# Attention and feed-forward in one kernel: casts, a shift of V and two V products placed at other half-steps

## The chip, the cores and the metric

The kernel runs on one core of a Trainium2 chip. The metric is the device time of the whole program in microseconds (us). A core has five engines that run side by side, each working off its own queue strictly in order: TensorE (PE, matmuls), VectorE (DVE), ScalarE (ACT), GpSimd (POOL, which also issues DMAs) and SyncE (SP, which only issues DMAs). They wait for one another through semaphores.

## What is computed

Sliding-window causal attention over 8 batches, 8 heads, 576 positions and head size 64, and behind it a feed-forward layer without residual:

```python
scores = scale * np.matmul(q, k.transpose(0, 1, 3, 2))
mask = (rel >= 0) & (rel < window)          # rel = query - key position, window = 64
attn = softmax(np.where(mask, scores, -1e9))
x = np.matmul(attn, v)                      # as 4608 tokens x 512
h = x @ w_in                                # 512 -> 2048
out = (h - np.tanh(h)) @ w_out              # 2048 -> 512
```

## The kernel before

**Attention.** Heads are worked on in pairs: pair g is pair g mod 4 of batch g // 4, so there are 32 of them, 4 to a batch. A window of 64 queries needs 128 keys, and a batch has 9 windows. Loads by POOL's DMA queue turn float32 into bf16 on their way (`kall`, `qall`, `vall`). For a pair, `cast` (L111) reorders k and q into `kb` and `qb`; PE transposes them (`tr_rows`, L264) and an engine copies the result out to `kt` and `qs`. `tile_scores` (L279) makes the scores in two groups of windows (5 and 4), ACT takes the exponential (`pt`), and, with "mask", DVE multiplies by the mask (L295). `tile_pv` (L297) multiplies by V, and DVE divides by the row sums (reciprocal L308, product L310, into `xs`). For later pairs `scores`, `masking`, `pv` (L328) and `norm` (L335) do the same with other tiles. `x_tr` turns `xs` into the token-last form `xT`. V takes its own road: `cast_v` (L159) into `vb`, nine DMAs `keys_v` (L163) from `vb` into the upper 64 partitions of the window tile `vw`, half of them issued by SP and half by POOL, and then a shift of the upper into the lower partitions, one window on (`shift_v`, L168; by DVE in two copies of 64x2080 elements, L171).

**Feed-forward.** Tokens go in 9 chunks of 512. For a chunk, 16 h products (`hp_mm`, L377, four matmuls 128x512 each) fill a PSUM bank each, ACT takes the tanh (L388), and `g_sub` (L391) subtracts on DVE into `gT` (L395), which frees the bank. In chunk 1 three banks serve in turn (`hp_bank`, L374), and the tanh output has three buffers: the fourth h product waits for the first one's subtraction. Four y products to a token tile (`yp_mm`, L407) and `y_out` finish the chunk.

**The order.** It is written out by hand on a time scale of half-steps h. The dictionary `OPS` gives each half-step at most one h or y product: chunk 0 has h product m at half-step 2m, chunk 1 at 32 + 2m, chunk 0's y parts are at 64 to 79. `at(h, fn, ...)` hangs attention work on a half-step. The loop at the end emits, for each h: the h or y product (PE and tanh), then the hung items in the order in which `at` named them, then the subtraction. Below, "gT m" is the subtraction of h product m of its chunk. The order of the calls is the order on every engine's queue; nothing is rescheduled.

The lines that matter here: `cast_v` of batch 1 (L524), the casts of pairs 4 to 11 (L527 to L562), `shift_dve` of batch 2 (L563), the row of pair 8 in the table of L536 to L541 (its four numbers are the half-steps of the k transpose, the q transpose and the two groups of scores), `tile_pv` of pairs 8 and 9 (L564, L565), and `pv` and `norm` of the loop over later pairs (L597, L599; for pair 10, a = 49).

Of the kernel before, what the change touches and what calls it, by code (L numbers as in the profile page):

```python
# [15 lines left out]
def kernel(  # L16
# [142 lines left out]
    def cast_v(b, pr, eng=nc.gpsimd):  # L159
        move(eng, vb[:, :, 2 * pr:2 * pr + 2, 0:D].rearrange("p e h d -> p h e d"),  # L160
             stage.pop((b, pr, "v")).rearrange("p h (e d) -> p h e d", d=D))

    def keys_v(b, j, eng=nc.sync):  # L163

        eng.dma_start(out=vw[b % 2][64:128, j].rearrange("p h c -> p (h c)"),  # L165
                      in_=vb[8 * j:8 * j + 8].rearrange("p e h c -> p e (h c)"))
# [274 lines left out]
    def at(h, fn, *args):  # L441
        items.setdefault(h, []).append((fn, args))
# [10 lines left out]
    V, A, G, Y = nc.vector, nc.scalar, nc.gpsimd, nc.sync  # L453
# [67 lines left out]

    at(0, lambda: nc.vector.memset(vw[1][0:64, 0], 0.0))
    at(0, lambda: nc.vector.memset(qT[1], 0.0))
    for pr, h in enumerate((1, 3, 5, 9)):  # L524
        at(h, cast_v, 1, pr, V)
    at(9, lambda: [keys_v(1, j, (G, Y)[j % 2]) for j in range(NJ)])
    at(8, cast_pair, 4, V)  # L527
    at(11, cast_pair, 5, V)
    at(9, load_v_all, 2)
    for g in 8, 9, 10, 11:  # L530
# [5 lines left out]
    for g, t, ka, qa, a, b, eng in ((4, (10, 11, 13, 14), 6, 7, (4, 5), (6, 7), V),  # L536
                                    (5, (13, 14, 16, 17), 2, 3, (4, 5), (6, 7), V),
                                    (6, (17, 18, 20, 22), 2, 3, (4, 5), (4, 5), A),
                                    (7, (20, 22, 24, 26), 3, 3, (4, 5), (4, 5), A),
                                    (8, (31, 32, 34, 36), 3, 5, (4, 5), (4, 5), A),  # L540
                                    (9, (37, 38, 42, 44), 3, 6, (4, 5), (4, 5), A)):  # L541
        at(t[0], tr_rows, g, "k", ka, eng)
        at(t[1], tr_rows, g, "q", qa, A)
        at(t[2], tile_scores, g, 0, a, "hide" if g < 8 else "mask")
        at(t[3], tile_scores, g, 1, b, "hide" if g < 8 else "mask")
# [4 lines left out]
    at(30, x_tr, 1, 1, 0, 4, 7, V)  # L550
    at(30, x_tr, 1, 1, 4, 9, 4, A)
    at(21, lambda: [cast_v(2, pr) for pr in range(NP)])
    at(21, cast_pair, 8, G)
    at(23, lambda: [keys_v(2, j, (G, Y)[j % 2]) for j in range(NJ)])
    at(33, cast_pair, 9, V)
    at(23, load_w_out, 0)
    at(23, load_w_out, 1)
    at(23, load_all, 3, "q")
# [1 line left out]
    at(23, load_v_all, 3)  # L560
    at(44, cast_pair, 10, G)
    at(50, cast_pair, 11, G)  # L562
    at(39, shift_dve, 2, 0, 4)  # L563
    at(44, tile_pv, 8, (6, 7))  # L564
    at(48, tile_pv, 9, (6, 7))  # L565
    at(53, x_tr, 2, 0, 0, 4, 6, V)
    at(55, x_tr, 2, 0, 4, 9, 7, A)
# [7 lines left out]
    for g in range(2 * NP + 2, B * NP):  # L575
        b, pr = divmod(g, NP)
        a = STEPS[b][pr] if b in STEPS else 8 * g - 36
        if b == B - 1:
            at(a - 28, pace, a - 28)
            at(a - 28, load, g, "q", G)  # L580
            at(a - 28, load, g, "k", G)
            at(a - 17, cast, g, "q")
            at(a - 16, cast, g, "k")
            at(a - 14, bounce, g, "q")
            at(a - 13, bounce, g, "k")
            at(a - 8, tr_dma, g, "q")
            at(a - 7, tr_dma, g, "k")
            at(a, spread, g)
        elif b > 2:
            at(a - 7, cast, g, "q")  # L590
            at(a - 5, cast, g, "k")
        if b < B - 1:
            at(a, tr, g, "q", 5 if g < 12 else 2 if g < 13 else 3, A, V)
            at(a + 2, tr, g, "k", 3, A)
        for i in range(3):
            at(a + 5 + 2 * i, scores, g, i, 4)
            at(a + 13 + i, pv, g, i)  # L597
        at(a + 11, masking, g)
        at(a + 15, norm, g)  # L599
        if g in TURNS:  # L600
            h0, b0, h1, b1 = TURNS[g]
            at(h0, x_tr, b, pr // 2, 0, 4, b0, V)
            at(h1, x_tr, b, pr // 2, 4, 9, b1, A)
        elif b > 3 and pr == NP - 1:
            at(a + 16, x_dma, b)
        if b > 2:
            cv, cs, ky = VALUES[b]
            at(cv + cs * pr, cast_v, b, pr)
        if pr == 0 and b > 2:
            for j in range(NJ):  # L610
                if b == 3:
                    at(ky, windows_v, b, j, (G, Y)[j % 2])
                else:
                    at(ky + j // 2 if b < 7 else ky + j, windows_v if b < 5 else keys_v, b, j, Y)
            if b > 4:
                at(ky + 7 if b < 7 else ky + 11, shift_v, b, 0, NJ - 1)
            if b == 3:
                continue
            hk, hq, hv = LOADS[b]
            for h, f in sorted(((hq, (load_all, b, "q")), (hk, (load_all, b, "k")), (hv, (load_v_all, b))),  # L620
                               key=lambda x: x[0])[2 if b == B - 1 else 0:]:
                at(h, pace, h)
                at(h, *f)
# [49 lines left out]
```

## Time and profile before

| what | value |
|---|---|
| median of five runs | 335.81 us (334.38 to 336.46) |
| the profiled execution's own time | 334.5 us |
| its span on the core | 332.8 us |
| PE busy | 315.4 us, 95% of the span |
| DVE busy | 198.7 us, 60% |
| ACT busy | 184.0 us, 55% |
| POOL busy | 114.8 us, 34% |
| 50 to 57 us: PE, DVE, ACT, POOL busy | 6.83, 5.06, 6.63, 7.00 of 7.00 us |
| 57 to 61 us: the same | 3.04, 3.94, 3.11, 4.00 of 4.00 us |
| 61 to 65 us: the same | 3.30, 3.97, 1.44, 1.53 of 4.00 us |

The profile is of one execution. Times in it count from the start of the span. A line of its timeline has the start, the duration, the engine, the source line and operation, the output and inputs, and in brackets how long the engine was idle before and who ended the wait.

### The profile page before, as it was taken

What the parts mean: (1) busy time and instruction counts of PE and PEld (TensorE: products, weight loads), DVE (VectorE), ACT (ScalarE), POOL (GpSimd) and SP (SyncE); (2) the same over time, 40 slices, a digit from 0 to 9 for tenths busy, and PEclk for the clock granted to TensorE, in tenths of its full rate; (3) what the DMA queues carried; (4) which work ended last, traced back from release to release, by engine and by line L of the source; (5) the groups of instructions that cost most, each with busy time, mean ns of one, the idle gap of its engine ahead of it and who ended that gap; (6) DMA issues with size and microseconds to landing.
All of it is one profiled execution on the core that took longest, in us unless ns stands there. A gap on an engine that the chain in (4) does not pass through costs nothing.

```text
span 332.8 us, 6238 instructions
## 1 busy us (share of the span) xinstructions
PE 315.4 (95%) x2408; PEld 176.5 (53%) x2439; DVE 198.7 (60%) x335; ACT 184.0 (55%) x337; POOL 114.8 (34%) x167
## 2 busy tenths in 40 slices
PE   6788999899999999999999999999999999999996
PEld 2564565465555655555555555555554444444444
DVE  4588597983257675767676666776666433344400
ACT  3545879583565666766556666555553444434411
POOL 8853589505920843532723493400000000000000
PEclk9569999999999999999999999999999999999999
DMA  8999996994797289475976968967104001100022
GB/s 159 166 194 207 165 187 104 200 194 97 123 194 143 44 153 224 90 113 130 166 134 115 156 146 162 199 145 166 63 32 102 34 32 42 53 33 32 32 84 77
DMA packets 47222, 40.68 MB, mean 122 GB/s; under 512 B 18632, under 2 KB 40584, under 8 KB 47000
## 3 DMA queue, kind: packets, MB, share of 16 engines
q0 software_dynamic: 21440, 19.73, 39.1%
q1 hardware_dynamic: 25544, 20.25, 24.1%
q8 instruction: 19, 0.31, 0.4%
q10 hardware_dynamic: 208, 0.29, 0.3%
q14 instruction: 11, 0.09, 0.1%
HBM read 36.70 MB, written 10.62 MB: 142 GB/s over the span
## 4 chain that ended last, share of the span: by engine, by line
PE 71%; DMA 10%; DVE 9%; POOL 3%; ACT 3%; issue 2%; POOLq 0%; DVEq 0%
PE ps L407 32%; PE ps L383 28%; DMA vall<-in_v_dram 4%; DMA vw<-vb 3%; DMA qall<-in_q_dram 3%; PE ps L332 3%; PE ps L316 3%; DVE gT L395 2%; DVE xs L343 2%; PE ps L249 2%; DVE qt L85 1%; PE ps L422 1%; DVE vw L171 1%; ACT qt L83 1%; POOL vb L85 1%
## 5 line engine op out<-in xcount | busy, mean ns | idle before, releaser
L383 PE MATMUL ps<-xT,wi 128*128 128x512 bf16 x576 | 147.1, 379 | 1.6 <-DVE gT L395 1.1
L395 DVE TENSOR_TENSOR gT<-ps,th 128x512 bf16<-128x512 f32 x144 | 98.4, 689 | 69.1 <-ACT th L388 67.8
L407 PE MATMUL ps<-w_out_sb,gT 128*128 128x512 bf16 x531 | 135.7, 379 | 1.5
L388 ACT ACTIVATE th<-ps 128x512 f32<-128x512 f32 x144 | 86.0, 599 | 81.6 <-PE ps L383 78.5
L383 PEld LDWEIGHTS <-wi 128*128 128x128 bf16 x576 | 60.5, 113 | 46.3 <-issue 3.2
L407 PEld LDWEIGHTS <-gT 128*128 128x128 bf16 x560 | 52.2, 98 | 52.7 <-issue 0.5
L318 ACT ACTIVATE pt<-ps 128x384 bf16<-128x384 f32 x66 | 32.3, 489 | 23.8 <-PE ps L316 23.8
L85 POOL COPY vb<-vall 72x1024 bf16<-72x1024 bf16 x24 | 24.7, 1052 | 35.2 <-DMA vall<-in_v_dram 30.9
L343 DVE TENSOR_TENSOR xs<-ps,rc 64x576 bf16<-64x576 f32 x44 | 33.2, 755 | 1.1
L412 ACT ACTIVATE ysb<-ps 128x512 f32<-128x512 f32 x35 | 21.0, 599 | 18.9 <-PE ps L407 18.8
L85 DVE COPY qt<-ps 64x576 bf16<-64x576 bf16 x18 | 13.7, 760 | 24.1 <-ACT qt L83 24.1
L85 POOL COPY qb<-qall 96x768 bf16<-96x768 bf16 x23 | 19.4, 844 | 20.5 <-DMA qall<-in_q_dram 18.9
L332 PEld LDWEIGHTS <-pt 128*128 128x128 bf16 x198 | 16.5, 98 | 15.9 <-DVE pt L322 0.8
L332 PE MATMUL ps<-vw,pt 128*128 128x130 bf16 x198 | 22.2, 220 | 0.9 <-DMA vw<-vb 0.5
L316 PE MATMUL ps<-qt,kt 128*128 128x128 bf16 x198 | 21.8, 219 | 0.0
L316 PEld LDWEIGHTS <-kt 128*128 128x128 bf16 x198 | 15.4, 98 | 8.8 <-issue 0.2
L85 POOL COPY kb<-kall 96x768 bf16<-96x768 bf16 x23 | 19.5, 848 | 0.7 <-DMA kall<-in_k_dram 0.7
L322 DVE TENSOR_TENSOR pt<-pt,ps 128x1152 bf16<-128x1152 bf16 x22 | 16.4, 744 | 0.8 <-ACT pt L318 0.8
L83 ACT ACTIVATE kt<-ps 128x576 bf16<-128x576 bf16 x22 | 14.4, 654 | 1.6 <-PE ps L249 1.5
L291 ACT ACTIVATE pt<-ps 128x640 bf16<-128x640 f32 (+1 forms) x20 | 12.5, 647 | 3.5 <-PE ps L288 3.5
L83 ACT ACTIVATE qt<-ps 64x576 bf16<-64x576 bf16 x18 | 11.5, 638 | 1.4 <-PE ps L249 1.4
L165 POOL DMA_DIRECT2D vw<-vb x17 | 10.2, 604 | 5.7 <-DVE vb L85 3.0
(76 smaller groups left out, 203.8 us busy)
## 6 DMA issues: line engine op xcount, KB each, us to landing
out_dram<-ysb SPq DMA_DIRECT2D x35, 256.0 KB
vall<-in_v_dram POOLq DMA_DIRECT2D x7, 576.0 KB, 12.3
vw<-vb SPq DMA_DIRECT2D x39, 65.0 KB
qall<-in_q_dram POOLq DMA_DIRECT2D x4, 576.0 KB, 12.6
kall<-in_k_dram POOLq DMA_DIRECT2D x4, 576.0 KB, 12.7
kall<-in_k_dram POOLq DMA_DIRECT2D x15, 144.0 KB, 6.0
qall<-in_q_dram POOLq DMA_DIRECT2D x15, 144.0 KB, 6.5
wi<-in_moe_w_in_dram POOLq DMA_DIRECT2D x2, 1024.0 KB, 13.1
```

What stands on the lines that cost most here:

```text
L83: nc.scalar.activation(o, i, ACT.Copy)
L85: eng.tensor_copy(o, i)
L316: nc.tensor.matmul(sp[:, i, :], kT[g % NK][:, 64 * j:64 * j + 128], qT[g % NR][:, :, 64 * j:64 * j + 64], start=True, stop=True)
L318: nc.scalar.activation(PT[g % NPT][:, 3 * grp:3 * grp + 3, :], sp, ACT.Exp, scale=scale)
L322: nc.vector.tensor_tensor(p, p, mask.unsqueeze(1).to_broadcast([128, 2 * NJ, 64]), ALU.mult)
L332: nc.tensor.matmul(ps[:, 5 + grp, 130 * i:130 * i + 130], PT[g % NPT][:, j, :], vw[b % 2][:, j, 2 * pr:2 * pr + 2, :], start=True, stop=True)
L343: nc.vector.tensor_tensor(xo[r, :, :, pr, :], ov[r, :, :, h, 0:D], rc[r].to_broadcast([64, 3, 3, 64]), ALU.mult)
L383: nc.tensor.matmul(hp, w_in_tile(ki, m), chunk_tile(c)[:, :, ki % 2, 64 * (ki // 2):64 * (ki // 2) + 64], start=(ki == 0), stop=(ki == 3))
L388: nc.scalar.activation(th, hp, ACT.Tanh)
L395: nc.vector.tensor_tensor(gT[c][:, m, :], hp, th, ALU.subtract)
L407: nc.tensor.matmul(yp, gT[c][:, m, s * 128:(s + 1) * 128], w_out_sb[:, m, :], start=(m == 0), stop=(m == M - 1))
L412: nc.scalar.activation(ysb, ps[:, yp_bank(c, s), :], ACT.Copy)
```

## The change

The cast of pair 4 goes from half-step 8 to 4, and the third of four casts of batch 1's V from 5 to 6. The cast of pair 8 goes from POOL at half-step 21 to DVE at 31, the cast of pair 9 from 33 to 35, and the two groups of scores of pair 8 with its transposes two half-steps later. The shift of batch 2's V goes from 39 to 38. The V product of pair 8 goes from 44 to 45, and the V products and the norm of pair 10 by one half-step.

```diff
-    for pr, h in enumerate((1, 3, 5, 9)):
+    for pr, h in enumerate((1, 3, 6, 9)):
         at(h, cast_v, 1, pr, V)
...
-    at(8, cast_pair, 4, V)
+    at(4, cast_pair, 4, V)
...
-                                    (8, (31, 32, 34, 36), 3, 5, (4, 5), (4, 5), A),
+                                    (8, (33, 34, 36, 38), 3, 5, (4, 5), (4, 5), A),
...
-    at(21, cast_pair, 8, G)
+    at(31, cast_pair, 8, V)
...
-    at(33, cast_pair, 9, V)
+    at(35, cast_pair, 9, V)
...
-    at(39, shift_dve, 2, 0, 4)
-    at(44, tile_pv, 8, (6, 7))
+    at(38, shift_dve, 2, 0, 4)
+    at(45, tile_pv, 8, (6, 7))
...
-            at(a + 13 + i, pv, g, i)
+            at(a + (14 if g == 10 else 13) + i, pv, g, i)
...
-        at(a + 15, norm, g)
+        at(a + (16 if g == 10 else 15), norm, g)
```

## The prediction

> **What bounds the kernel now.** I read the page's first lines, then the list of waits, then the timeline where TensorE (PE) stands still.
>
> ```profile
> PE 315.4 (95%) x2408; PEld 176.5 (53%) x2439; DVE 198.7 (60%) x335; ACT 184.0 (55%) x337; POOL 114.8 (34%) x167
> PE   6788999899999999999999999999999999999996
> ```
>
> PE is the bound over the whole; an edit is worth only the PE idle time that it removes or makes. All moved work lies between 27 and 82 us, so I looked there. Two waits of PE from the list:
>
> ```profile
> PE ps L304 <- DVE vw L171: 0.9, 1, 0.9
> PE ps L332 <- DMA vw<-vb: 0.5, 1, 0.5
> ```
>
> The first timeline stretch, early in chunk 0:
>
> ```profile
> 30.15 0.35 DVE L85 COPY kb<-kall 96x768 bf16<-96x768 bf16 x1
> 30.55 0.43 PE L269 MATMUL ps<-ident,kb 96*128 96x96 bf16 x6 [1.11 <-DVE kb L85]
> ...
> 31.42 1.02 PE L383 MATMUL ps<-xT,wi 128*128 128x512 bf16 x4 [0.17 <-DVE gT L395]
> ```
>
> PE idles 1.11 us for pair 4's cast, but what comes next waits for a gT subtraction anyway. From 27.34 to 34.76 VectorE (DVE) works without a gap. The second stretch holds the shift of V and what runs beside it:
>
> ```profile
> 57.34 1.24 POOL L135 DMA_DIRECT2D vall<-in_v_dram  x1
> 57.49 3.24 DVE L171 COPY vw<-vw 64x2080 bf16<-64x2080 bf16 x2
> ...
> 58.56 0.84 POOL L85 COPY kb<-kall 96x768 bf16<-96x768 bf16 x1
> ...
> 59.33 0.83 POOL L85 COPY qb<-qall 96x768 bf16<-96x768 bf16 x1
> ...
> 60.10 1.31 POOL L85 COPY kb<-kall 96x768 bf16<-96x768 bf16 x1
> 60.76 0.69 DVE L395 TENSOR_TENSOR gT<-ps,th 128x512 bf16<-128x512 f32 x1
> 60.78 0.35 PE L304 MATMUL ps<-vw,pt 128*64 128x65 bf16 x10 [0.86 <-DVE vw L171]
> ...
> 61.37 1.17 POOL L85 COPY qb<-qall 96x768 bf16<-96x768 bf16 x1
> ...
> 61.51 2.02 PE L383 MATMUL ps<-xT,wi 128*128 128x512 bf16 x8 [0.37 <-DVE gT L395]
> ```
>
> The two copies of the shift take 3.24 us here; in the instructions on tile vw the same copy has a minimum of 697 and a maximum of 2618 ns. The slow one runs beside GpSimd's (POOL's) casts of pairs 10 and 11. PE pays 0.86 + 0.37 us, and 0.33 at 63.85 for the first V product's output (DVE xs L310). From 50.7 to the h product of half-step 50 (64.56) PE loses 2.87 us: 13.86 elapsed less 10.99 of work at the spacings of the timeline (0.865 for four 128x512 matmuls, 0.26 for six transposes or ten score matmuls, 0.22 for eight, 0.47 for a V product).
>
> [...] 2.62 us for a 0.70 copy, and POOL casts of 1.31 and 1.17 against 0.83 beside the copy's end and a mask multiply. [...] the vall issue took 1.24 against 0.85 us elsewhere.
>
> **The change part by part.** The order of the built program shows what moves on each queue; SP's is the same. Sums are made against the profiled execution, 334.5 us (span 332.8, 1.7 around it); the median of the runs is 335.81, 1.3 higher, so I add the difference to the median.
>
> *Early casts (pair 4 from 8 to 4, V's third from 5 to 6).* The same DVE work before the same gT: pair 4 goes ahead of gT 2, vb 2 and gT 3. Its casts would start at 28.62 and 28.89; q's load was issued at 16.75 and took 12.0, so it is there at 28.8. kb is ready 1.5 us sooner, PE's transposes fill a hole, but the h matmul after them still waits for the gT ending at 31.37, and V's last cast still ends at 31.70, so POOL's and SP's V windows start as before. Later the last of pair 7's loads holds DVE to 40.0 in either order. Gain 0, cost 0. That cover is thin by 0.1 us at q's load; a late load would cost what it is late, up to 0.3, the PE wait at 41.07 that stands anyway.
>
> *Cast of pair 8 from POOL to DVE, scores of pair 8 two half-steps later.* POOL loses 0.82 + 0.82 (0.77 spacing each, about 1.5 us). Everything behind on its queue starts 1.5 us sooner: five V windows, two w_out loads, three whole-batch loads, then the casts of pairs 10 and 11. DVE gains 0.35 + 0.36 where it idles 1.23 us (51.5 to 52.7): hidden. But these copies and those of pair 9, now at 54.4, fall on POOL's DMA issues and hold them (an L165 issue at 32.60 beside such copies took 1.02 against 0.59), say 0.4 in all. So POOL's first late cast starts at 58.56 - 1.5 - 0.4 (the vall issue not held now) + 0.4 = about 57.1, and its four run to about 60.2.
>
> *The shift from 39 to 38.* It now stands ahead of gT 3 and gT 4 on DVE, but behind pair 8's second mask multiply, which has itself moved two half-steps. Laid out: h product 38 ends 56.05, tanh 56.7, exp of the second scores 57.2, mask 57.2 to 57.6, shift from 57.53. It was 57.49: no sooner. Unhindered it ends 58.86. Queued behind it now are gT 3, 4, 5 and both masks of pair 9; h product 44 needs gT 3's bank and waits from 58.35. If S is the shift's end: that product starts S + 0.65, pair 9's second scores and exp follow, mask S + 2.8, gT 6, then the first V product's output (it now stands behind gT 6, 0.6 us) ends S + 4.85, the second V product starts, and h product 50 comes at S + 5.6. Before it came at 64.56 = 60.73 + 3.83. So PE is level if S = 58.95, and each us later costs a whole us.
>
> [...] Bound below: [...] S = 58.86, -0.1. Bound above: POOL's first cast is ahead of the mask, two casts go to 58.65, then DVE and POOL alternate (mask 0.35, cast 0.77, copy 0.62, cast 0.77, copy 0.62): S = 61.8, +2.85. Before, a copy that asked at 58.11 got in only at 60.1, behind the rest of a DMA issue and two whole casts. If the mask slips in ahead of the first cast and that repeats for the copies, the first runs from 58.65 to 59.3, waits out one cast, and the second ends at S = 60.7, +1.75. The two starts (57.1, 57.2) are nearer than I can tell; I take S = 61.1 between the two orders, +2.15.
>
> *Products of pair 10 a half-step later.* PE waited 0.36 us at 73.07 for the mask; 0.17 us of score matmuls go ahead of them now: -0.2. The norm moves behind one more y part (0.87); nothing of DVE's waits on it before 77.4: 0.
>
> *Sooner loads.* The V windows of batch 3 hang on its load of V (landed 78.7), queued behind the w_out loads. About 1 us sooner, or PE later, and the 0.53 us wait at 99.3 is gone: -0.53. I take it whole.
>
> Sum: 0 + 2.15 - 0.2 - 0.53 = +1.4 us: 335.9 for the profiled execution, 337.2 for the median.
>
> **The rivals.** (a) *Shift undisturbed*: POOL's casts come late or DVE is served first, S = 58.86: -0.1 - 0.2 - 0.53 = -0.8, 335.0. For it: the starts on both engines lie within 0.4 us of each other. Against it: at three boundaries between POOL's instructions the waiting copy won only the last. This is the mechanism on the other side: it decides below S = 59.7, where the sum changes its sign. (b) *The early hole is regained too*: the 1.11 us at 30.55 become work, 335.0 - 1.1 = 333.9. Against it: the gT at 31.37 and the loads to 40.0. (c) *Full collision and nothing given back*: S = 61.8, and DMA issues held so that the wait at 99.3 stays: +2.85 - 0.2 = +2.65, 338.5. For it: each is the end of a bound; against it: both must happen. That the order isn't changed as described can't be: the built order shows it.
>
> **How the numbers follow.** The five runs of this kernel scatter by 0.6%, so about 0.5% (1.7 us) is what can be told from no change. Forecast (collision, S = 60.0 to 61.8, so +0.3 to +2.1, with 0.5 of scatter): 0.58, of it 0.27 above 1.7. Rival (a) 0.22, of it 0.10 with more regained than worked out (over 1.7). (b) 0.08, faster. (c) 0.12, slower. Faster 0.10 + 0.08 = 0.18, same 0.31 + 0.12 = 0.43, slower 0.27 + 0.12 = 0.39. The forecast's own range is 336.1 to 338.0. The range 334.7 to 338.5 takes in (a) and reaches (c); it leaves out (b), the better part of (a) and the upper half of (c) with its scatter, near 0.2.
>
> **What would show it.** Right: the shift starts near 57.5 and takes over 2.5 us beside POOL casts that start near 57; h product 44 waits for gT over 2 us; pair 8's cast at 51.4 without a stall; no wait at 99. Wrong: shift of 1.4 us, or one that starts before 57; a gap at 30 that closes and stays closed past 41; PE losing under 2.9 us between 50.7 and h product 50.

## The result and the profile after

The changed kernel takes 341.37 us (median of 25 runs, 335.8 to 346.67) against 335.85 (44 runs, 333.75 to 339.04). The ratio of the compared runs is 1.0085, 95% interval 1.006 to 1.0111: slower, and above the range of the prediction by its median. The ratio is smaller than that of the medians (1.016) because the comparison leaves out runs more than 1.5% above a kernel's fastest, which for the changed kernel is 14 of the 25.

The profiled execution after took 340.35 us, its span is 338.6 (before: 334.5 and 332.8). The page's first line and TensorE's slices, with the clock granted to it below them:

```profile
PE 318.9 (94%) x2408; PEld 177.6 (52%) x2439; DVE 199.3 (59%) x337; ACT 184.2 (54%) x337; POOL 113.9 (34%) x165
PE   7877998599999999999999999999999999999996
PEclk9999799899999999999999999999999999999999
```

PE has the same 2408 matmuls and yet is busy for 3.5 us longer; slice 8 of PE (59 to 68 us) fell to 5, and the clock row shows a 7 and an 8. So PE stands idle there, and some matmuls run slower (the 7 is at 34 to 42 us, the 8 at 59 to 68). Where the 5.8 us of span went, by the starts of certain h products (the L383 groups of the timeline; "hp 30" is that of half-step 30):

| stretch | before, us | after, us | difference |
|---|---|---|---|
| span start to hp 0 | 24.00 | 24.41 | +0.41 |
| hp 0 to hp 30 | 25.06 | 26.59 | +1.53 |
| hp 30 to hp 50 | 15.50 | 20.24 | +4.74 |
| hp 50 to chunk 2's first | 25.47 | 25.31 | -0.16 |
| chunk 2's first to the end | 242.77 | 242.07 | -0.70 |

The third row is the result. The list of waits after, from 50 to 72 us (who waits, for whom; us in total, times, longest):

```profile
PE ps L383 <- DVE gT L395: 4.2, 1, 4.2
DVE vw L171 <- DMA vw<-vb: 2.4, 1, 2.4
```

The first line is the wait foreseen: h product 44, for the subtraction behind the shift. The second was not: the shift itself waits for a DMA, a window of V. VectorE's timeline after, at that place:

```profile
56.31 0.98 DVE L85 COPY kb<-kall 96x768 bf16<-96x768 bf16 x1
57.21 0.97 DVE L85 COPY qb<-qall 96x768 bf16<-96x768 bf16 x1
58.11 0.47 DVE L295 TENSOR_TENSOR pt<-pt,mask_sb 128x640 bf16<-128x640 bf16 x1
58.50 0.68 DVE L395 TENSOR_TENSOR gT<-ps,th 128x512 bf16<-128x512 f32 x1
59.80 0.51 DVE L295 TENSOR_TENSOR pt<-pt,mask_sb 128x512 bf16<-128x512 bf16 x1 [0.62 <-ACT pt L291]
60.34 1.21 DVE L171 COPY vw<-vw 64x2080 bf16<-64x2080 bf16 x1
63.93 0.70 DVE L171 COPY vw<-vw 64x2080 bf16<-64x2080 bf16 x1 [2.38 <-DMA vw<-vb]
```

The first copy takes 1.21 us beside POOL's casts, not 2.6; the second, at 63.93, has waited 2.38 us for its window and then runs undisturbed in 0.70. The shift ends at 64.63.

Why does the window come late? The windows are issued by SP and POOL. SP's and POOL's timeline before:

```profile
49.96 2.82 SPq L165 DMA_DIRECT2D vw<-vb  x4
...
49.88 0.82 POOL L85 COPY kb<-kall 96x768 bf16<-96x768 bf16 x1
50.65 0.82 POOL L85 COPY qb<-qall 96x768 bf16<-96x768 bf16 x1
51.42 2.92 POOL L165 DMA_DIRECT2D vw<-vb  x5
54.32 1.49 POOL L188 DMA_DIRECT2D w_out_sb<-in_moe_w_out_dram  x2
```

and after:

```profile
50.90 4.23 SPq L165 DMA_DIRECT2D vw<-vb  x4
...
51.17 2.91 POOL L165 DMA_DIRECT2D vw<-vb  x5 [0.30 <-POOL vb L85]
54.06 1.49 POOL L188 DMA_DIRECT2D w_out_sb<-in_moe_w_out_dram  x2
```

Before, the cast of pair 8 kept POOL busy until SP's first two windows were out, and SP's four took 2.82 us. Without it both issue at once, and SP needs 4.23. The instructions on tile vw, after (durations in ns as minimum/median/maximum, then first and last start):

```profile
L165 POOL DMA_DIRECT2D vw<-vb x5: 558/594/643, 51.2 to 53.4; - x5
L165 SPq DMA_DIRECT2D vw<-vb x4: 604/898/1527, 50.9 to 53.9; - x4
```

SP's last window leaves at 53.9, 3.0 us after its first, where 2.1 us separated them before, and 0.13 us later POOL issues the first of two 1024 KB loads of w_out. The DMA queues show which window is late. From 57 to 63.9 us (packets, MB, share of the 16 DMA engines' time; q0 is POOL's queue, q1 is SP's):

```profile
q0 software_dynamic: 293, 1.13, 95.0%
q1 hardware_dynamic: 72, 0.07, 3.6%
```

SP's four windows are 288 packets in all. The last 72 of them, one window's worth, are still on their way here, beside POOL's packets, which take 95.0% of the DMA engines' time. Before, none of SP's packets is left after 56 us. So the second copy can start only at 63.93, ten us after that window was issued.

The third effect is behind the stall. PE's timeline after, and then the busy time of each engine by stretch (window, length; PE, PEld, DVE, ACT and POOL busy with the number of instructions; the granted clock; DMA share; GB/s):

```profile
65.40 1.87 PE L383 MATMUL ps<-xT,wi 128*128 128x512 bf16 x4 [4.20 <-DVE gT L395]
...
71.24 1.03 PE L383 MATMUL ps<-xT,wi 128*128 128x512 bf16 x4
```

```profile
61.00:65.00 4.00, 0.20 (x10) 0.20 (x7) 1.59 (x3) 1.19 (x2) 1.23 (x1) 1.00 1.06 212
65.00:68.50 3.50, 3.10 (x33) 1.43 (x33) 1.97 (x5) 1.08 (x2) 0.00 (x0) 0.51 1.08 207
68.50:72.00 3.50, 3.19 (x38) 1.89 (x37) 3.43 (x7) 1.75 (x3) 0.00 (x0) 1.00 1.31 197
```

From 61 to 65 us PE works for 0.20 us. For 3.4 us after the stall TensorE has half its clock (0.51 in the second row, 1.00 in the others): four matmuls take 1.87 us, and 1.03 at 71.24.

### The profile page after: what moved, and what is told of

Read it like the earlier page. It is cut to its first block, busy times and chain, and to the rows that moved or that the text cites. A ratio compares the mean times of both kernels' runs of the same rounds, so it can differ in the third digit from the quotient of the medians.

```text
span 338.6 us, 6241 instructions
## 1 busy us (share of the span) xinstructions
PE 318.9 (94%) x2408; PEld 177.6 (52%) x2439; DVE 199.3 (59%) x337; ACT 184.2 (54%) x337; POOL 113.9 (34%) x165
## 4 chain that ended last, share of the span: by engine, by line
PE 75%; DMA 9%; DVE 8%; ACT 3%; POOL 2%; issue 2%; POOLq 0%; DVEq 0%; ACTq 0%
PE ps L407 33%; PE ps L383 30%; DMA vall<-in_v_dram 4%; PE ps L332 3%; DMA vw<-vb 3%; PE ps L316 3%; DVE xs L343 2%; DVE gT L395 2%; PE ps L249 2%; DMA qall<-in_q_dram 2%; DVE qt L85 2%; ACT qt L83 1%; PE ps L422 1%; PE ps L269 1%; POOL vall L143 1%
## 5 line engine op out<-in xcount | busy, mean ns | idle before, releaser
L383 PE MATMUL ps<-xT,wi 128*128 128x512 bf16 x576 | 148.9, 383 | 7.6 <-DVE gT L395 6.5
L383 PEld LDWEIGHTS <-wi 128*128 128x128 bf16 x576 | 60.6, 114 | 53.0 <-issue 9.8
L85 POOL COPY qb<-qall 96x768 bf16<-96x768 bf16 x22 | 18.7, 850 | 21.9 <-PE ps L349 12.7
L96 POOL DMA_DIRECT2D qall<-in_q_dram x15 | 10.0, 666 | 6.1 <-DMA wi<-in_moe_w_in_dram 3.6
```

The source lines that it names most:

```text
L85: eng.tensor_copy(o, i)
L383: nc.tensor.matmul(hp, w_in_tile(ki, m), chunk_tile(c)[:, :, ki % 2, 64 * (ki // 2):64 * (ki // 2) + 64], start=(ki == 0), stop=(ki == 3))
```

## The experiments

The theories, as they stood when the runs were made: the *port* (the shift takes longer where casts of pairs 10 and 11 run beside it, as predicted; a name alone, for what a profile shows is the time, as before 2.62 us for a copy of 0.70), and as rival the *window* (the sooner POOL queue makes SP's last window late). The first run asks whether the early casts cost time. Each run is timed beside the kernel before: medians, then the ratio of the compared runs with its 95% interval.

**The parts by themselves.** Early casts alone, on the kernel before:

```diff
-    for pr, h in enumerate((1, 3, 5, 9)):
+    for pr, h in enumerate((1, 3, 6, 9)):
-    at(8, cast_pair, 4, V)
+    at(4, cast_pair, 4, V)
```

> The kernel before with the two early edits alone (pair 4 cast at 4, V's third cast at 6). Theory of the window DMA (the loss comes from pair 8's cast leaving GpSimd): no change, within 0.5 us of before. Rival, the early casts: in the changed kernel's profile PE is already 1.9 us late at h product 30 (51.0 against 49.1), so this kernel is 1.5 to 2.5 us slower, with the half-clock stretch of PE near 34 us.

Measured: 335.75 against 335.94, ratio 0.9981 (0.9948 to 1.0014). No cost and no gain that can be told; the rival's 1.5 to 2.5 us did not come.

The cast of pair 8 and the row alone, on the kernel before:

```diff
-                                    (8, (31, 32, 34, 36), 3, 5, (4, 5), (4, 5), A),
+                                    (8, (33, 34, 36, 38), 3, 5, (4, 5), (4, 5), A),
-    at(21, cast_pair, 8, G)
+    at(31, cast_pair, 8, V)
-    at(33, cast_pair, 9, V)
+    at(35, cast_pair, 9, V)
```

> The kernel before with pair 8's cast on VectorE at 31, pair 9's at 35 and pair 8's transposes and scores two half-steps later; the shift stays at 39 and everything else as before. Theory of the window DMA: most of the loss is here, 2 to 4 us slower, and SyncE's fourth window lands after 60 us, with the shift's second copy waiting for it. Rival, port collision of the shift with GpSimd's casts 10 and 11: loss of about 1 to 2 us, the shift takes over 3 us and no wait for a window DMA shows.

Measured: 339.44 against 335.94, 1.0059 (1.0027 to 1.0091). VectorE's shift in this kernel:

```profile
58.78 2.48 DVE L171 COPY vw<-vw 64x2080 bf16<-64x2080 bf16 x1
65.04 0.70 DVE L171 COPY vw<-vw 64x2080 bf16<-64x2080 bf16 x1 [3.78 <-DMA vw<-vb]
```

The first copy takes 2.48 us beside POOL's casts, as one of the two copies takes 2.62 before. The second one's wait for a window is new; PE waits 4.16 us behind it, and SP's issues took 4.39 us. No other part of the change is in this kernel, so the late window comes with the cast and the row.

The shift and the later products alone, on the kernel before:

```diff
-    at(39, shift_dve, 2, 0, 4)
-    at(44, tile_pv, 8, (6, 7))
+    at(38, shift_dve, 2, 0, 4)
+    at(45, tile_pv, 8, (6, 7))
-            at(a + 13 + i, pv, g, i)
+            at(a + (14 if g == 10 else 13) + i, pv, g, i)
-        at(a + 15, norm, g)
+        at(a + (16 if g == 10 else 15), norm, g)
```

> The kernel before with the shift at 38, pair 8's V product at 45 and pair 10's products a half-step later; casts as before. The shift can start at about 56.8, when the last window lands, 0.7 us sooner, and its copies are done before GpSimd's casts start at 58.5. Window DMA theory: faster by 0.5 to 1.5 us. Port theory: the same or more, since the collision is avoided. Early theory: no change from these edits.

Measured: 336.88 against 335.94, 0.999 (0.9955 to 1.0026): nothing that can be told, where a gain of 0.5 to 1.5 us was expected. The shift meets no cast here and takes 1.94 us in place of 3.24, but a mask of pair 9 takes 1.09 in place of 0.48, and PE waits 1.24 us for a subtraction and 0.71 for a V product's output. With pair 8's masks left where they were, an earlier shift does neither good nor harm.

**Window or port?** The changed kernel with the cast of pair 8 back on POOL, ahead of POOL's windows:

```diff
-    at(31, cast_pair, 8, V)
+    at(21, cast_pair, 8, G)
```

> The changed kernel with the cast of pair 8 back on GpSimd at 21, all other edits kept. Theory of the window DMA: the windows land before 57.5 us again and nearly all of the loss is gone, within 1 us of before. Port collision: GpSimd's casts are back at 58.5, the shift at 57.5 to 60.7, so also near before plus 1 us. Early casts: 1.5 to 2.5 us stay.

Measured: 339.02 against 335.94, 1.0077 (1.0053 to 1.0101). SP's issues are back at 2.82 us and no copy waits for a window, yet the loss is there, against the expectation of both theories. (The early casts, which were to leave 1.5 to 2.5 us here, cost nothing by themselves above.) Its timeline:

```profile
58.28 3.72 DVE L171 COPY vw<-vw 64x2080 bf16<-64x2080 bf16 x2
...
58.56 0.88 POOL L85 COPY kb<-kall 96x768 bf16<-96x768 bf16 x1
...
59.33 0.87 POOL L85 COPY qb<-qall 96x768 bf16<-96x768 bf16 x1
...
60.09 1.35 POOL L85 COPY kb<-kall 96x768 bf16<-96x768 bf16 x1
...
62.77 1.72 PE L383 MATMUL ps<-xT,wi 128*128 128x512 bf16 x4 [3.84 <-DVE gT L395]
```

That is the collision with the casts alone: the shift starts at 58.28 and ends at 62.00, and PE waits 3.84 us for what is queued behind it. So removing the window's cause does not cure the change; the moved row of pair 8, with the shift behind its second mask, is enough for the collision.

The changed kernel with all nine windows of batch 2 on POOL:

```diff
-    at(23, lambda: [keys_v(2, j, (G, Y)[j % 2]) for j in range(NJ)])
+    at(23, lambda: [keys_v(2, j, G) for j in range(NJ)])
```

> The changed kernel with all nine V windows of batch 2 issued by GpSimd, so that the w_out loads stand behind every window on one queue. Window theory: no window lands after 59 us and the 2.4 us wait of the shift's second copy is gone. Port theory: GpSimd's casts of pairs 10 and 11 now start near 60, the shift at about 59 to 60 still meets DMA issues and casts. If only the window mattered, the loss against before falls from 5.5 to under 1.5 us; if the port matters too, 2 to 4 us stay.

Measured: 339.0 against 335.91, 1.0072 (1.0043 to 1.01). No copy of the shift waits for a window (it took 2.00 us), but POOL's queue is 2.2 us longer: its casts now meet pair 9's mask (1.85 us at 63.19 in place of 0.48; PE waits 1.82, 0.30 and 0.92), and the wait for the next batch's window at 102 is back with 0.93 us.

**Window in time, shift held less or not.** The changed kernel with pair 10's cast ahead of the w_out loads, so that it stands between POOL's windows and those loads and is done when the shift comes:

```diff
+    at(23, cast_pair, 10, G)
     at(23, load_w_out, 0)
...
-    at(44, cast_pair, 10, G)
```

> The changed kernel with the cast of pair 10 ahead of the w_out loads on GpSimd. The loads go out 1.55 us later, as before the change, and by the rotation of the row buffers pair 11's cast then waits for pair 10's transposes, so no GpSimd cast stands beside the shift. Window theory: windows land by 58 us. Port theory: the shift meets only DMA issues of GpSimd, 1.4 to 2.2 us. Together: PE loses under 1.5 us at h product 44 and the whole comes to before, within 1 us, or better by up to 0.8.

Measured: 336.56 against 335.91, 1.002 (0.9997 to 1.0043). The instructions on tile vw in this kernel, SP's windows and the shift:

```profile
L165 SPq DMA_DIRECT2D vw<-vb x4: 604/897/1542, 51.1 to 54.2; - x4
L171 DVE COPY vw<-vw x2: 1316/1342/1369, 59.7 to 61.0; 64x2080 bf16<-64x2080 bf16 x2
```

SP's issues are as slow as in the changed kernel (4.24 us), but the last leaves 1.6 us ahead of the first w_out load (55.83) instead of 0.13, and nobody waits for it. The shift's copies are held less (1.32 and 1.37 us), though pair 11's casts, at 59.69 and 60.46, do stand beside them, which was not expected; PE waits 2.43 us. So the slow issue went with a late window where the first load came 0.13 us behind SP's last window, and with none late where it came 1.6 us behind: here the second copy starts at 61.0, right behind the first.

The kernel with the cast of pair 8 on POOL, and POOL made to wait for a subtraction (a copy of one element of gT, L447) ahead of the casts of pairs 10 and 11:

```diff
-    at(31, cast_pair, 8, V)
+    at(21, cast_pair, 8, G)
...
+    at(40, pace, 40)
     at(44, cast_pair, 10, G)
```

> The kernel of the third experiment (changed kernel, pair 8's cast on GpSimd), with a one-element GpSimd copy that waits for gT 3 (the first subtraction behind the shift) put ahead of the casts of pairs 10 and 11, so that these cannot run beside the shift. Port theory: the shift takes 1.4 to 2.2 us (DMA issues may still touch it) instead of 3.7, PE's wait at h product 44 falls from 3.84 to 1.2 to 2 us, the half-clock stretch behind it goes, and the loss falls from 3.1 us to under 1. If the place of the shift in the order is what costs, the loss stays near 3.

Measured: 336.4 against 335.91, 1.0004 (0.9982 to 1.0025). The shift takes 1.31 us at 58.23, PE's waits are 1.14 and 1.13, and the clock stays whole (1.00 from 49 to 72 us). Against the same kernel without the pacing (1.0077) the collision at the shift is worth about 0.7%.

**Pacing the kernel before.** Its shift is held too, so POOL is made to wait there ahead of the same casts:

```diff
+    at(42, pace, 42)
     at(44, cast_pair, 10, G)
```

> The kernel before with the same copy, waiting for gT 4 (the first subtraction behind the shift there), ahead of the casts of pairs 10 and 11. Port theory: the shift takes 1.4 us instead of 3.24 and PE's waits of 0.87 and 0.37 us at 60 to 61.5 go: 1 to 1.8 us faster than before, or less if pair 10's cast then comes late for its transposes at half-step 49. If the port is not it, no change.

Measured: 337.69 against 335.91, 1.0056 (1.0032 to 1.008): worse. Its timeline:

```profile
61.98 0.82 POOL L85 COPY kb<-kall 96x768 bf16<-96x768 bf16 x1
...
62.52 2.86 DVE L295 TENSOR_TENSOR pt<-pt,mask_sb 128x512 bf16<-128x512 bf16 x1
62.75 0.81 POOL L85 COPY qb<-qall 96x768 bf16<-96x768 bf16 x1
...
63.51 0.81 POOL L85 COPY kb<-kall 96x768 bf16<-96x768 bf16 x1
...
64.28 0.81 POOL L85 COPY qb<-qall 96x768 bf16<-96x768 bf16 x1
```

The shift is free (1.57 us), but the four casts now fall on a mask multiply of pair 9, which takes 2.86 us where its like takes 0.42 to 0.44. It ends at 65.38, behind the last of the four casts (65.09), and none of these is slowed (0.81 to 0.82); PE then waits 2.67 us, and half the clock follows that too (a mean of 0.62 from 65 to 68.5 us). The changed kernel with all windows on POOL and the pacing of half-step 40:

```diff
-    at(23, lambda: [keys_v(2, j, (G, Y)[j % 2]) for j in range(NJ)])
+    at(23, lambda: [keys_v(2, j, G) for j in range(NJ)])
...
+    at(40, pace, 40)
     at(44, cast_pair, 10, G)
```

> The changed kernel with both suspects taken away: all V windows of batch 2 issued by GpSimd, and the one-element copy that waits for gT 3 ahead of GpSimd's casts of pairs 10 and 11. If the late window and the port are the whole loss, the two gains add up: 339.0 - 2.6, so 336.4 or less, level with before, and no half-clock stretch after 50 us. If something else costs (the shift's new place ahead of gT 3), 1.5 us or more stay.

Measured: 338.52 (four runs) against 336.5, 1.0077 (1.0051 to 1.0103). That is a miss, and for the reason just seen: the shift took 1.57 us and no window was late, but the casts met pair 9's first mask, 3.12 us at 61.47, and PE waited 1.39, 1.57 and 0.90.

**A better order?** Three kernels on the kernel before: pair 10's cast ahead of the w_out loads (the edit shown above); batch 3's load of V ahead of its q and k; and both.

```diff
+    at(23, load_v_all, 3)
     at(23, load_all, 3, "q")
     at(23, load_all, 3, "k")
-    at(23, load_v_all, 3)
```

> The kernel before with pair 10's cast ahead of the w_out loads on GpSimd, so that the shift meets no cast. Port theory: the shift takes 1.4 to 2 us and the waits at 60 to 61.5 (1.24 us) shrink to under 0.4. But the w_out loads and batch 3's load of V behind them go out 1.55 us later, so the wait for batch 3's windows (0.53 us at 99.3) grows by up to 2 us. Net between 1 us faster and 1 us slower. A rival that the port is not the cause sees the shift at over 3 us.

> The kernel before with batch 3's load of V ahead of its loads of q and k on GpSimd. Batch 3's windows come 3 to 5 us sooner, so the 0.53 us wait at 99.3 goes: 0.5 us faster at most; nothing changes at 57 to 64 us. If that wait is of no account, no change.

> The kernel before with both: pair 10's cast ahead of the w_out loads, and batch 3's load of V ahead of q and k. If the port costs before about 1.2 us and the wait at 99.3 another 0.5, this one is 1.2 to 1.8 us faster than before. If the sum comes out at no change, what the shift gains is lost again on another wait, which the profile must show.

Measured against 336.5: 336.76, 1.0025 (1.0004 to 1.0046); 335.98, 0.9981 (0.9957 to 1.0005); 335.57, 0.9993 (0.9974 to 1.0013). With the earlier cast the shift takes 2.22 us instead of 3.24, but two masks of pairs 8 and 9 go from under 0.5 to 1.15 and 0.92. The sooner load of V takes the wait at 99 away (none in the second kernel, 0.24 in the third). None beats the kernel before by what can be told; in the first and third the masks lose what the shift gains (1.1 us against 1.0).

## Why the prediction was wrong

Its sign and its main mechanism were right (a held shift, PE waiting at h product 44 for over 2 us); the size was not. That the wait came out in the changed kernel is in part luck, since there a late window, which the prediction did not have, held the shift longest. 337.2 was said; 341.37 came, and the compared runs alone put 335.81 x 1.0085 = 338.7, still above the range.

*The step that failed: the cast of pair 8.* The prediction put "Everything behind on its queue starts 1.5 us sooner: five V windows, two w_out loads" and followed that only to the casts at the end of the queue. It did not ask what the sooner issues would fall on at its head. They fell on SP's issues (2.82 to 4.23 us), and the packets of POOL's loads on those of SP's last window (293 beside 72 from 57 to 63.9 us), which the prediction put at nothing. SP's order is the same, as the prediction said, but its times are not. In the hp 30 to hp 50 stretch S, the end of the shift, was to come 61.1 - 49.06 = 12.04 us after hp 30 and came at 64.63 - 51.00 = 13.63: 1.59 us from this. Of the 4.74 us of the stretch, 2.15 are the size that was predicted, 1.59 the later S, and 1.0 is the next point. That is a sum for this profile, not what the window costs by itself: with its cause taken away (cast 8 back on POOL) the ratio is 1.0077 in place of 1.0085, since the shift then runs beside the casts (3.72 us) instead. S comes 12.52 us after hp 30 there, and the stretch is still 18.99 us, 3.49 more than before.

*The term left out: the clock.* From S to hp 50 the prediction counted 5.6 us; it was 71.24 - 64.63 = 6.61. The one us more is the stretch at half clock: the four matmuls of h product 44 alone take 0.84 more (1.87 for 1.03). The kernel with the shift and the later products alone has the same order behind the shift and takes 1.02 us for that product, and its S to hp 50 is 5.72.

In the changed kernel's profile each of the two stretches at half clock behind a wait lasts 3.41 us (34.34 to 37.75 and 65.06 to 68.47). It is 3.4 us too after the 3.84 us stall in the run with the cast back on POOL, and after 2.43 with pair 10's cast first (worked out from the mean clock of 61 to 68.5 us). TensorE's busy time in 3.41 us, in the first four rows just ahead of a stretch at half clock, in the others over waits that none followed:

| stretch | PE busy of 3.41 us | clock behind it |
|---|---|---|
| changed kernel, 61.65 to 65.06 | 0.00 | half |
| changed kernel, 30.93 to 34.34 | 1.67 | half |
| pair 10's cast first, 59.97 to 63.38 | 0.98 | half |
| before, paced, 62.43 to 65.84 | 1.31 | half |
| all windows on POOL, 61.20 to 64.61 | 1.88 | whole |
| cast 8 on POOL, paced, 61.39 to 64.80 | 2.46 | whole |
| all windows on POOL, paced, 63.70 to 67.11 | 1.02 | whole |

In the four stretches ahead of half the clock TensorE was busy for 0 to 49%, but the last row's 30% was followed by the whole clock (1.00 from 61 to 72 us). Nor does the length of one wait tell them apart: half the clock followed one of 1.47 us (changed kernel, 31.05 to 32.52), and none one of 1.82 (all windows on POOL). What decides is not shown.

*The collision of the shift (+2.15).* It is shown by the kernel with cast 8 back on POOL and its paced copy: 3.72 us for the shift beside the casts, 1.31 without them. In the changed kernel itself the casts begin at 57.91, 6.91 us after hp 30 (8.0 was forecast), and hold the masks and copies less than was laid out (1.21 us for the first copy): the mask ahead of the shift came only at 59.80, since VectorE's own copies of pair 9 took 0.98 and 0.97 us beside POOL's issues of loads at 56.31 and 57.08, where they take 0.35. The prediction had charged that meeting to POOL alone. Had the window been there, the second copy would have been next at 61.55, beside a POOL cast that runs from 60.94 for 1.29 us; so in this profile the window, not the casts, ended last. With it in time S would have been near 62.8 (an estimate: that cast's end, and 0.56 us as for the second copy with the cast back on POOL), 11.8 us after hp 30 and near the forecast. The two stand in for each other: with the window in time but VectorE held as much elsewhere the ratio stays at 1.007 to 1.008 (three kernels), and with the window in time and the shift held less or not, 1.002 and 1.0004. No run has the late window without casts beside the shift.

*Early casts, 0:* right by time (0.9981). In the profile after, hp 0 to hp 30 took 1.53 us more. Of this 1.12 lies from hp 14 to hp 16, at half clock (2.98 us; 1.86 before, at whole clock, and 1.84 with the cast back on POOL), and 0.66 from hp 8 to hp 10, where a cast of V waits 0.76 us for its load; that stretch scatters from 0.86 to 1.69 us with the early casts and from 0.86 to 1.42 without. The half clock there may still owe something to them. The hole did close, but the h product behind the transposes then waited 1.47 us for its gT in one piece (before, PE waited 1.11 and 0.17). With the early casts alone it waited 1.13, with the cast back on POOL 1.37, and the h products behind that took 1.02 to 1.05 us in both, where one took 1.91 at half clock in the changed kernel.

*Cast of pair 8 on VectorE, hidden:* right, it ran at 53.34 in 0.35 us. It also took away a wait that the profile before doesn't show: in five of the nine profiles with this cast on POOL, PE waited 0.2 to 1.8 us for it (1.72 with the shift and the later products alone, where POOL's queue ahead of it had waited 5.45 us for the load of V). *Products of pair 10, -0.2:* right, -0.16, and every kernel with this edit has 25.31 in that stretch. *Sooner loads, -0.53:* right in size, no wait for a window at 99 to 103, and -0.70 from chunk 2's first to the end. Which of the two reasons given did it is open. In the changed kernel both hold: its load of V is issued 6.1 us after hp 30 (before: 8.3), and hp 50 comes 4.74 later. In the kernel with the shift and the later products alone hp 50 is later too (17.04 us after hp 30, before: 15.50), but the load is later still, issued 6.6 us ahead of hp 50 (before: 7.2). The wait is gone there as well, with the same 242.07; the load took 20.3 us in place of 21.4.

*Rivals.* (a), an undisturbed shift, was refuted by the wait of 4.20. (b), the early hole regained, shows in no run. (c), full collision, came nearest in size, but not in its reasons: what was to be given back was given back.

## What to carry to other kernels

When work is taken off a queue that issues DMAs, write down for each DMA behind it what the other queue issues at its new time, the first ones above all: a gap that looked like waste may have kept two issuers apart. A run of POOL casts fell on something of VectorE's wherever these runs put it; look for a place beside its subtractions from PSUM (0.68 us at 58.50 after, beside a cast, as ever), not for one that merely frees the instruction that hurts today. Before a stall is priced, ask what the clock does behind it: between 50 and 72 us here, 3.4 us at half clock (6.8 with the cast and the row alone) followed each of the five waits of 2.43 to 4.20 us, and in the changed kernel that made about one us more.

## What the runs showed of the hardware

- Beside a POOL run of four casts, masks of 0.42 and 0.48 us took 2.86 and 3.12 and ended behind the last cast (at 65.38 for 65.09, and at 64.59 for 64.24), none of the casts slowed (0.81 to 0.82). Neither got in between two casts. Elsewhere VectorE did: a mask got in after one cast with the shift and the later products alone (1.09 us), the shift's copy after two with the cast back on POOL (2.48 us; it ended ahead of the third, which took 1.35 us) and after three with the cast and the row alone (2.48). What decides is open.
- VectorE's copies took 0.98 and 0.97 us beside POOL's issues of loads, for 0.35. It isn't so each time: before, the copies at 53.32 and 53.59 took 0.35 and 0.36 beside POOL's issues of windows.
- SP's four issues took 2.82 us where the first of POOL's five of the same kind came 1.46 us after SP's first, and 4.23 to 4.39 where it came 0.27 us after; the third and the fourth were the slow ones (1.53 and 1.19 us for 0.60 and 0.70). Beside only three of POOL's, at 31.73 before, four took 2.55.
- A window of 65 KB issued 0.13 us ahead of two loads of 1024 KB on the other queue was awaited for ten us; issued 1.6 us ahead it was in time. From 57 to 63.9 us 293 packets of POOL's queue passed beside the window's 72, about four for each of its own; no run shows why.
